# Attention over channels, then top-128 routing: batch 2's update taken before batch 3's gather, a weight load split unevenly, and a window of three on batch 3's stores

## The chip, the cores and the metric

The program runs on one core of one Trainium2 chip. The metric is the device time of one execution in microseconds (us). Before the change it is 260.9 us, the median of three runs (260.78 to 260.98). TensorE is PE in the rows, VectorE DVE, ScalarE ACT, GpSimd POOL, SyncE SP. DMAs are issued by POOL (loads, gathers, scatters) and by SP (weights, stores), and 16 DMA engines carry them.

## What is computed

Four batches of 6208 rows by 256 columns. For each batch the columns of q and k are scaled to length one, a 256x256 softmax is taken of the product of k and q over the rows, and v is multiplied by it. Then 128 rows of the result are chosen by a score and changed by a small MLP:

```python
qn = q / (norm(q, axis=1) + 1e-6);  kn = k / (norm(k, axis=1) + 1e-6)
a = softmax(kn.transpose(0, 2, 1) @ qn / tau)          # 256 x 256 for each batch
x = v @ a                                              # 6208 x 256
scores = x @ w_gate
for b in range(4):
    top = the 128 rows with the highest scores[b]
    ye = maximum(x[b, top] @ w1, 0) @ w2               # w1 256x1024, w2 1024x256
    out[b, top] = x[b, top] + sigmoid(scores[b, top]) * ye
```

All other rows of the output are x.

## The kernel before

Each batch is cut into six chunks of 1024 rows (128 partitions of 8 rows) and a rest of 64 rows, in the order 0, rest, 1 to 5. One chunk of q, k or v is a 1 MB load, cast to bf16 on the way. Batches are numbered 0 to 3; the code calls batch 2 `E` and batch 3 `L`. A batch passes through these steps:

- p1: matmuls over q and k give the norms (`p1_norms`, line 390, tile `g_ps`) and the product (`p1_rows`, line 401, `s_ps`); then the softmax (`softmax_stages`).
- T, S, O: each half chunk of v is transposed (`p2_transpose`, line 500, `vt_ps`), scored (`p2_score`, line 547, `sc_ps`) and multiplied by the softmax (`p2_out`, line 581; two rows a matmul group, copied to `stage` by ACT at line 599).
- Select: seven rounds on DVE and PE narrow a threshold (`select_stages`, lines 655 to 682), then the 128 row numbers come out (`idx`, line 735), POOL gathers those rows of v (line 741), PE transposes them (line 765, tile `vg`), the MLP runs (lines 775 to 830), and POOL scatters `upd` into the output (line 844). The scatter has to wait until the stores of its batch have landed.
- Two chunks of batch 2 (`LATE`, chunks 4 and 5) are treated otherwise: their O runs at the very end, with the MLP's change added by two more matmuls (line 588), so they need no scatter. Their stores wait for batch 2's scatter.

The order of the instructions is set at build time by a planner (the `while True` loop from line 942), which keeps model times for the engines (`Engines`) and the DMA queues (`Rings`) and takes, at each step, the ready piece of lowest priority number: chains (softmax, select, MLP), then S, then p1 and T, then O. Where PE would be idle, it puts in dummy matmuls (`unread`, line 533). A chain that has gathered asks `calm` whether it may go on; a chain that wants to scatter waits for `("stored", b)`. Stores that are ready before the loads have been issued are kept in `deferred`; the first of them waits for the load `GATE`, the first half of batch 3's last v chunk, and the others stand behind it in SP's order (lines 960 to 969). Each engine runs its instructions in the order written. DMAs of SP and of POOL each take turns over eight semaphores, so each waits for the landing of the one eight places ahead of it.

The w1, w2 and gate weights are loaded by SP at the start (lines 275 to 278) and cast by ACT once (lines 944 to 956).

Of the kernel before, what the change touches and what calls it, by code (L numbers as in the profile page):

```python
# [17 lines left out]
P = 128  # L18
# [7 lines left out]
FAR = 1.0e9  # L26
# [84 lines left out]
def kernel(  # L111
# [12 lines left out]
    nc = tc.nc  # L124
# [20 lines left out]
    VT_BUFS = 13  # L145
    AHEAD = 12.0

    const = ctx.enter_context(tc.tile_pool(name="const", bufs=1))
# [57 lines left out]
    def now():  # L206
        return eng.t["pe"]
# [51 lines left out]
    def pump():  # L259
        rings.run(now())  # L260
        flying[:] = [key for key in flying if rings.done.get(key, FAR) > now()]
        while nxt_unit[0] < len(units):
            u = units[nxt_unit[0]]
            if not slots[bucket(u)] or sum(length[key] for key in flying) >= AHEAD:
# [11 lines left out]
                      in_=moe_w1.rearrange("(dc p) f -> p dc f", p=P))  # L276
    nc.sync.dma_start(out=w2_st, in_=moe_w2.rearrange("(p fc) d -> p fc d", p=P))
    nc.sync.dma_start(out=wg_row, in_=moe_w_gate[None, :])
# [72 lines left out]
    late_add = []  # L351
    scatter_inst = {}
    gathered = set()
    softmaxes = [0]
# [265 lines left out]
    def select_stages(b, dep):  # L620
# [173 lines left out]
        sf = eng.dve(C, xf, extra=0.16)  # L794
        yield ("t", f)
        h_sb = moe.tile([P, NFC, P], BF16, name="h_sb")
        hfs = []
# [55 lines left out]
    def calm(b):  # L853
        if b == L:
            return True
        if b == E:
            return acc_dead[0]
        if softmaxes[0]:
            return False
        if acc_dead[0]:  # L860
            return True
        if not queue["T"]:
            return True
        u, g = queue["T"][0]
        return g != gs[0] or u not in loaded or rings.landing(arrival_key[u + (3,)]) > now() + 6.0

    class Chain:
# [7 lines left out]
        def ready(self):  # L875
            if self.need[0] == "t":
                return self.need[1]
            if self.need[0] == "dma":
                return rings.landing(self.need[1]) if calm(self.b) else FAR
            b = self.need[1]  # L880
            if held[b]:
                return FAR
            if b == L:
                return now()
            return max(rings.landing(key) for key in stored[b]) + (0.5 if L in gathered else 3.0)

# [30 lines left out]
    def stage_ready():  # L917
# [5 lines left out]
        return rings.landing(("st",) + key)  # L923

    def out_store(b, ci):
        dep = stage_done[(b, ci)]
# [5 lines left out]
        for h in range(parts):  # L932
            key = ("st", b, ci) if h == parts - 1 else ("st", b, ci, h)
            issued = eng.issue("sp", 0.42, dep)
            rings.add(1, issued + 0.65, STORE / parts + 0.009 if ci < NFULL else 0.2, key, 0.45)
            ins = emit_store(b, ci, h, parts)
        stored[b].append(key)
        if not late(b, ci):
# [3 lines left out]
    while True:  # L942
        pump()
        if not cast_done and now() > 8.0:
            w1v = w1_st.rearrange("p a c -> p (a c)").rearrange("p (dc m fc) -> p dc fc m", dc=C // P, fc=NFC)
# [11 lines left out]
        if nxt_unit[0] == len(units) and not drained and E in gathered:  # L957
            nc.gpsimd.drain(fusable=False)
            drained = True
        if deferred and GATE in load_inst:  # L960
            for b, ci in sorted(deferred, key=lambda d: -d[0]):
                st = out_store(b, ci)
                if not gate_done:
# [4 lines left out]
                        reason="stores behind the last loads")  # L968
            deferred = []
        t = now()  # L970
# [41 lines left out]
        if late_phase() and (queue["p1"] or queue["T"]):  # L1012
            coming = min([a[0] for a in able if a[1] == 2] + [FAR])
            fit = [a for a in fit if a[1] < 3 or coming > t + 0.44 + EARLY]
        if acc_dead[0]:
# [48 lines left out]
        else:  # L1064
# [8 lines left out]
            if out_at == len(outs) or outs[out_at][1][0] != g[0]:  # L1073
                if back(b, g[0]) and not gate_done:
                    deferred.append((b, g[0]))
                else:
                    out_store(b, g[0])
# [35 lines left out]
```

## Time and profile before

| | us |
|---|---|
| time, median of 3 | 260.9 |
| the profiled execution's own time | 260.56 |
| its span | 258.5 |
| PE busy | 214.4 (83%) |
| ACT busy | 94.5 |
| DVE busy | 98.9 |

HBM read 78.91 MB and written 25.95 MB. The span is the time from the program's first to its last instruction, 2.06 us less than the execution. The program can be read in three stretches: loads with the stores of batches 0 and 1 among them, up to about 217 us; stores of batches 1, 2 and 3 up to 255 us; and the last scatter with the end of the program. In a row of a timeline the columns are the start, the duration, engine, line, operation, the tiles written and read, the shape, the count, and in brackets how long the engine had been idle and what released it. A busy PE is not a PE at its peak, and a DMA share above 1 means that packets of one DMA engine overlap in the records.

### The profile page before, as it was taken

Reading aid. Unit: us, or ns where it says so; the run is one execution under the profiler, and the core shown is the slowest. Engines: PE = TensorE matmul, PEld = TensorE weight load, DVE = VectorE, ACT = ScalarE, POOL = GpSimd, SP = SyncE. Lnnn points to the kernel's source line nnn. Section 1 sums busy time; section 2 is a strip of 40 time slices with the busy share of each in tenths; the row PEclk is TensorE's granted clock in tenths of the full one; section 3 lists DMA queues with packets and bytes.
Section 4 is the critical chain, followed back from the end, with each engine's and each line's share of the span. In section 5 each row is a group of like instructions: output and inputs, shape, how many; then the busy total and the mean of one; then the engine's idle time right before and its main releaser. Section 6 shows DMA issues by size and latency. Waiting matters only on the chain.

```text
span 258.5 us, 8230 instructions
## 1 busy us (share of the span) xinstructions
PE 214.4 (83%) x3668; PEld 175.5 (68%) x3668; DVE 98.9 (38%) x417; ACT 94.5 (37%) x173; POOL 56.5 (22%) x105
## 2 busy tenths in 40 slices
PE   0396866898998995997958999899999889999960
PEld 0265655795876674786736788787878779887840
DVE  0200004367450055443663033556555256766030
ACT  2800004800116565457400021811022087698610
POOL 8241212223104110130104322123205300010201
PEclk9999799569999997999985999999999999999996
DMA  7999999999999999999999999999999996999995
GB/s 239 256 216 213 214 214 214 214 212 213 213 213 295 311 363 318 257 281 295 364 241 213 212 214 212 214 212 212 214 213 210 211 212 171 411 423 412 394 411 235
DMA packets 16852, 66.97 MB, mean 259 GB/s; under 512 B 2097, under 2 KB 3634, under 8 KB 13618
## 3 DMA queue, kind: packets, MB, share of 16 engines
q0 software_dynamic: 12528, 38.93, 75.5%
q1 hardware_dynamic: 4290, 27.53, 26.4%
q8 instruction: 28, 0.46, 0.6%
q14 instruction: 6, 0.05, 0.0%
HBM read 78.91 MB, written 25.95 MB: 406 GB/s over the span
## 4 chain that ended last, share of the span: by engine, by line
PE 48%; DMA 37%; DVE 6%; ACT 4%; issue 2%; POOLq 1%; POOL 0%; SPq 0%; DVEq 0%
DMA q_ch<-in_q_dram 17%; PE s_ps L401 12%; DMA k_ch<-in_k_dram 10%; PE o_ps L581 8%; PE g_ps L390 8%; DMA v_ch<-in_v_dram 7%; PE sc_ps L533 4%; DMA out_dram<-stage 3%; PE m_ps L673 3%; PE vt_ps L500 2%; PE sc_ps L547 2%; ACT stage L599 2%; PE s_ps L581 2%; DVE cmp L655 1%; PE g_ps L581 1%
## 5 line engine op out<-in xcount | busy, mean ns | idle before, releaser
L599 ACT COPY stage<-o_ps 128x512 f32<-128x512 f32 x78 | 43.8, 589 | 64.1 <-PE o_ps L581 62.9
L401 PE MATMUL s_ps<-q_ch,k_ch 128*128 128x256 bf16 x384 | 50.9, 287 | 0.0
L401 PEld LDWEIGHTS <-k_ch 128*128 128x128 bf16 x384 | 36.8, 102 | 6.3
L581 PE MATMUL o_ps<-a_sb,vt_sb 128*128 128x256 bf16 (+1 forms) x270 | 39.0, 274 | 2.6 <-ACT stage L599 2.5
L581 PEld LDWEIGHTS <-vt_sb 128*128 128x128 bf16 (+1 forms) x294 | 26.6, 98 | 8.9 <-issue 4.9
L500 PE MATMUL vt_ps<-ident_b,v_ch 128*128 128x128 bf16 x336 | 26.8, 236 | 2.8 <-DMA v_ch<-in_v_dram 1.9
L390 PE MATMUL g_ps<-q_ch 128*64 128x64 bf16 x768 | 18.5, 202 | 12.0 <-DMA q_ch<-in_q_dram 12.0
L500 PEld LDWEIGHTS <-v_ch 128*128 128x128 bf16 x384 | 25.1, 105 | 4.2 <-DMA v_ch<-in_v_dram 2.5
L390 PEld LDWEIGHTS <-q_ch 128*64 128x64 bf16 x768 | 15.1, 116 | 17.6 <-DMA q_ch<-in_q_dram 13.0
L415 DVE SCALAR_TENSOR_TENSOR junk<-g_ps,ident_h 128x64 f32<-128x64 f32 x16 | 3.6, 225 | 57.9 <-PE g_ps L390 57.5
L243 POOL DMA_DIRECT2D q_ch<-in_q_dram x25 | 13.9, 556 | 44.8 <-DMA q_ch<-in_q_dram 9.6
L519 DVE COPY vt_sb<-vt_ps 128x1024 bf16<-128x1024 bf16 x24 | 15.9, 689 | 20.1 <-PE vt_ps L500 20.1
L390 PE MATMUL g_ps<-k_ch 128*64 128x64 bf16 x768 | 18.1, 201 | 6.2 <-DMA k_ch<-in_k_dram 6.2
L390 PEld LDWEIGHTS <-k_ch 128*64 128x64 bf16 x768 | 15.0, 116 | 10.3 <-DMA k_ch<-in_k_dram 7.2
L243 POOL DMA_DIRECT2D v_ch<-in_v_dram x25 | 13.6, 546 | 34.6 <-DMA q_ch<-in_q_dram 19.2
L533 PE MATMUL sc_ps<-w_sb,ident_b 128*128 128x256 bf16 x134 | 20.3, 277 | 0.4 <-DVE sc L626 0.4
L243 POOL DMA_DIRECT2D k_ch<-in_k_dram x25 | 13.7, 547 | 28.8 <-DMA v_ch<-in_v_dram 13.4
L410 ACT COPY s_sb<-s_ps 128x512 f32<-128x512 f32 x4 | 2.3, 586 | 45.0 <-PE s_ps L401 45.0
L655 DVE SCALAR_TENSOR_TENSOR cmp<-sc,wl,tab 128x392 bf16<-128x392 f32 x28 | 17.5, 626 | 1.0
L844 POOL DMA_INDIRECT out_dram<-upd,idx x4 | 4.0, 997 | 49.3 <-DMA out_dram<-stage 49.0
L547 PEld LDWEIGHTS <-vt_sb 128*128 128x128 bf16 (+1 forms) x294 | 10.8, 100 | 5.0 <-issue 2.3
L547 PE MATMUL sc_ps<-aw_sb,vt_sb 128*128 128x2 bf16 (+1 forms) x294 | 11.7, 166 | 2.7 <-DVE aw_sb L479 2.6
(176 smaller groups left out, 261.4 us busy)
## 6 DMA issues: line engine op xcount, KB each, us to landing
out_dram<-stage SPq DMA_DIRECT2D x18, 1024.0 KB, 11.0
q_ch<-in_q_dram POOLq DMA_DIRECT2D x23, 512.0 KB, 16.9
k_ch<-in_k_dram POOLq DMA_DIRECT2D x23, 512.0 KB, 16.3
v_ch<-in_v_dram POOLq DMA_DIRECT2D x23, 512.0 KB, 17.8
out_dram<-stage SPq DMA_DIRECT2D x12, 512.0 KB, 8.9
stage<-in_moe_w_dram SPq DMA_DIRECT2D x2, 1024.0 KB, 5.0
q_ch<-in_q_dram POOLq DMA_DIRECT2D x2, 256.0 KB
k_ch<-in_k_dram POOLq DMA_DIRECT2D x2, 256.0 KB, 15.6
```

The lines of the kernel that those rows point to most:

```text
L243: ins = nc.gpsimd.dma_start(out=t[:, rows, :], in_=lview(src, b, d)[:, rows, :])
L390: nc.tensor.matmul(g_ps[h * H:(h + 1) * H, 2 * which + cc, :], lhsT=x, rhs=x, start=d == FIRST and s == 0 and cc == 0 and which == 0, stop ...
L401: nc.tensor.matmul(s_ps[:, cc, :], lhsT=kt[:parts, s, cc * P:(cc + 1) * P], rhs=qt[:parts, s, :], start=d == FIRST and s == 0 and cc == 0, ...
L500: nc.tensor.transpose(vt_ps[:, cc, j, :parts], in_=vt[:parts, v0 + j, cc * P:(cc + 1) * P], identity=ident_b[:parts, :parts])
L519: nc.vector.tensor_copy(vt_sb[:, :, :n, :parts], vt_ps[:, :, :n, :parts])
L533: nc.tensor.matmul(t[:, 256:512], lhsT=ident_b, rhs=w1_sb[:, 0, 0:256], start=not sc_open[0], stop=not sc_open[0])
L547: nc.tensor.matmul(sc_ps[:parts, col, :], lhsT=vt_sb[:, cc, j, :parts], rhs=aw_sb[:, cc, :], start=cc == 0 and col == 0, stop=cc == 1 and ...
L581: nc.tensor.matmul(o_ps[:parts, pj, :], lhsT=vt_sb[:, cc, j, :parts], rhs=a_sb[:, cc, :], start=pj == 0 and cc == 0, stop=last and cc == 1 ...
L599: nc.scalar.copy(st[:parts, rows, :], o_ps[:parts, :m, :])
L655: nc.vector.scalar_tensor_tensor(out=cmp, in0=sc[:, :, None].to_broadcast([P, NCOL, NTHR]), scalar=wl[:, i, NTHR:NTHR + 1], in1=tab[:, Non ...
L673: nc.tensor.matmul(mps[:, 0:7 * NTHR], lhsT=ones_b, rhs=cmp[:, 7 * h:7 * h + 7, :].rearrange("p s j -> p (s j)"), start=h == 0, stop=h == 6)
L844: ins = nc.gpsimd.indirect_dma_start(out=out_flat[0:(b + 1) * N, :], out_offset=bass.IndirectOffsetOnAxis(ap=idx[:, 0:1], axis=0), in_=upd ...
```

## The change

Five edits, all in the planner or at the start:

- The w2 load (1 MB) becomes one DMA of the first four of each partition's eight rows, and 16 DMAs of the other four rows with 8 partitions each (every fourth of 32 partitions). The planner puts the weights' casts at its 14 us instead of 8.
- `calm` lets batch 2's chain go on as soon as its gather has landed. A new stop, `("dead", f)`, holds it in front of the MLP's first weight until batch 3's p1 is done.
- Deferred stores are issued batch 2 first; batch 1's two follow when all of batch 2's (but the two late ones) have been issued.
- A batch before batch 2 doesn't scatter ahead of batch 3's gather once all loads are out; the allowance after the stores' landing is 1.5 us in the model for all.
- From the fourth on, each half store of a full chunk of batch 3 waits for the landing of the one three places ahead (`few`, `FEW = 3`, `after`).

```diff
+    UNEVEN = 4
...
-    nc.sync.dma_start(out=w2_st, in_=moe_w2.rearrange("(p fc) d -> p fc d", p=P))
+    w2v = moe_w2.rearrange("(p fc) d -> p fc d", p=P)
+    nc.sync.dma_start(out=w2_st[:, 0:NFC - UNEVEN], in_=w2v[:, 0:NFC - UNEVEN])
+    for p0 in [a + j for j in range(4) for a in range(0, P, P // 4)]:
+        ps = slice(p0, p0 + P // 4 - 3, 4)
+        nc.sync.dma_start(out=w2_st[ps, NFC - UNEVEN:], in_=w2v[ps, NFC - UNEVEN:])
...
         yield ("t", f)
+        if b == E:
+            yield ("dead", f)
         h_sb = moe.tile([P, NFC, P], BF16, name="h_sb")
...
         if b == E:
-            return acc_dead[0]
+            return True
...
+            if self.need[0] == "dead":
+                return self.need[1] if acc_dead[0] else FAR
...
-            return max(rings.landing(key) for key in stored[b]) + (0.5 if L in gathered else 3.0)
+            if b < E and L not in gathered and nxt_unit[0] == len(units):
+                return FAR
+            return max(rings.landing(key) for key in stored[b]) + 1.5
...
+    def after(later, earlier, reason):
+        tc.add_manual_dep(
+            later.ins, earlier.ins.name,
+            mybir.DependencyInfo(mybir.DependencyClass.Sync, mybir.DependencyReason.DATA), reason=reason)
...
             key = ("st", b, ci) if h == parts - 1 else ("st", b, ci, h)
+            if b == L and ci < NFULL and len(few) >= FEW:
+                dep = max(dep, rings.landing(few[-FEW][1]))
...
             ins = emit_store(b, ci, h, parts)
+            if b == L and ci < NFULL:
+                if len(few) >= FEW:
+                    after(ins, few[-FEW][0], "few stores at a time ahead of the last gather")
+                few.append((ins, key))
...
-        if not cast_done and now() > 8.0:
+        if not cast_done and now() > 14.0:
...
-        if deferred and GATE in load_inst:
-            for b, ci in sorted(deferred, key=lambda d: -d[0]):
+        if deferred and GATE in load_inst and (held[E] == 0 or any(b == E for b, _ in deferred)):
+            for b, ci in [d for d in deferred if d[0] == E] or list(deferred):
+                deferred.remove((b, ci))
                 st = out_store(b, ci)
...
-            fit = [a for a in fit if a[1] < 3 or coming > t + 0.44 + EARLY]
+            early = EARLY if not acc_dead[0] or len(queue["T"]) <= 3 else 0.0
+            fit = [a for a in fit if a[1] < 3 or coming > t + 0.44 + early]
...
-                if back(b, g[0]) and not gate_done:
+                if b < E and back(b, g[0]) or back(b, g[0]) and not gate_done:
                     deferred.append((b, g[0]))
```

What this does to the order is shown at three places. The first is SP's beginning, the weights; `stage` is their staging tile. Before:

```order
L275 DMA stage<-in_moe_w_dram 128x2x1024
L277 DMA stage<-in_moe_w_dram 128x2048
L278 DMA wg_row<-in_moe_w_gate_dram 1x256
L611 DMA out_dram<-stage 128x2048
L613 DMA out_dram<-stage_rem 64x256
```

Now:

```order
L276 DMA stage<-in_moe_w_dram 128x2x1024
L279 DMA stage<-in_moe_w_dram 128x1024
L282 DMA stage<-in_moe_w_dram 8x1024 x16
L283 DMA wg_row<-in_moe_w_gate_dram 1x256
L618 DMA out_dram<-stage 128x2048
```

The gate's row `wg_row` now stands behind 18 DMAs instead of two.

The second place is SP behind the last loads. The first row is batch 2's chunk 0, whose wait on `DMASW1` is the load `GATE`; `stage_2262` and `stage_2361` are batch 1's last two chunks before the change, `stage_2278` and `stage_2377` after it; 64x2048 is a half store of batch 3. Before:

```order
L611 DMA out_0_dram<-stage_3387 128x2048 [waits DMAHW7_49,DMASW1_49,Activation_49]
L613 DMA out_0_dram<-stage_rem_3876 64x256 [waits DMAHW0_49,Activation_49]
L611 DMA out_0_dram<-stage_3881 128x2048 [waits DMAHW1_49,Activation_49]
L611 DMA out_0_dram<-stage_2262 128x2048 [waits DMAHW2_49]
L611 DMA out_0_dram<-stage_2361 128x2048 [waits DMAHW3_49]
L611 DMA out_0_dram<-stage_4201 128x2048 [waits DMAHW4_49,Activation_49]
L611 DMA out_0_dram<-stage_4550 128x2048 [waits DMAHW5_49,Activation_49]
L611 DMA out_0_dram<-stage_4608 64x2048 [waits DMAHW6_49,Activation_49]
L611 DMA out_0_dram<-stage_4608 64x2048 [waits DMAHW7_49]
```

Now:

```order
L618 DMA out_0_dram<-stage_3897 128x2048 [waits DMAHW1_49,Activation_49]
L618 DMA out_0_dram<-stage_4232 128x2048 [waits DMAHW2_49,Activation_49]
L618 DMA out_0_dram<-stage_4483 128x2048 [waits DMAHW3_49,Activation_49]
L618 DMA out_0_dram<-stage_2278 128x2048 [waits DMAHW4_49]
L618 DMA out_0_dram<-stage_2377 128x2048 [waits DMAHW5_49]
L618 DMA out_0_dram<-stage_4606 64x2048 [waits DMAHW6_49,Activation_49]
L618 DMA out_0_dram<-stage_4606 64x2048 [waits DMAHW7_49]
L620 DMA out_0_dram<-stage_rem_4649 64x256 [waits DMAHW0_49,Activation_49]
L618 DMA out_0_dram<-stage_4669 64x2048 [waits DMAHW1_49,Activation_49]
L618 DMA out_0_dram<-stage_4669 64x2048 [waits DMAHW6_49,DMAHW2_49]
L618 DMA out_0_dram<-stage_4709 64x2048 [waits DMAHW7_49,DMAHW3_49,Activation_49]
```

Batch 2's four full chunks now go ahead of batch 1's two, and from the fourth half store of batch 3 each has a second DMA wait, on the half store three places ahead.

The third place is the end of POOL's order. The number of rows tells the scatters apart: 12416 is batch 1, 18624 batch 2, 24832 batch 3; the last `vg` is batch 3's gather. Before:

```order
L243 DMA v_ch<-in_v_dram 128x1024 x2
L844 DMA out_dram<-upd,idx 12416x256
L741 DMA vg<-in_v_dram,idx 128x256
L844 DMA out_dram<-upd,idx 18624x256
L844 DMA out_dram<-upd,idx 24832x256
```

Now:

```order
L244 DMA v_ch<-in_v_dram 128x1024 x2
L853 DMA out_dram<-upd,idx 18624x256
L748 DMA vg<-in_v_dram,idx 128x256
L853 DMA out_dram<-upd,idx 12416x256
L853 DMA out_dram<-upd,idx 24832x256
```

Batch 2's scatter now stands in front of batch 3's gather, and batch 1's behind it. On PE, batch 2's transposes of line 765 move ahead of the last eight matmuls of line 401, and between batch 3's last select matmul (line 727) and its line 765 there now stand seven O groups of batch 3 and seven late O groups of batch 2, where eight late O groups of batch 2 and twelve dummy matmuls stood before; the eighth late O group now comes right behind line 765.

## Rows read from the trace of the kernel before

**Rows 1.** The page: span, and DMA busy tenths in 40 slices.

```profile
span 258.5 us, 8230 instructions
...
DMA  7999999999999999999999999999999996999995
```

**Rows 2.** The page: the chain that ended last, by engine.

```profile
PE 48%; DMA 37%; DVE 6%; ACT 4%; issue 2%; POOLq 1%; POOL 0%; SPq 0%; DVEq 0%
```

**Rows 3.** Windows around the last loads; last three columns: PE clock, DMA share, GB/s.

```profile
213.00:214.00 1.00, 1.00 (x16) 0.94 (x15) 0.80 (x4) 1.00 (x2) 0.00 (x0) 1.00 1.08 211
214.00:215.00 1.00, 1.00 (x21) 1.00 (x19) 0.87 (x2) 1.00 (x3) 0.00 (x0) 1.00 0.64 129
215.00:216.00 1.00, 1.00 (x28) 0.96 (x27) 0.42 (x1) 1.00 (x4) 0.00 (x0) 1.00 0.62 113
216.00:217.00 1.00, 1.00 (x29) 0.95 (x29) 0.24 (x2) 0.69 (x3) 0.00 (x0) 1.00 0.57 107
217.00:218.00 1.00, 1.00 (x21) 0.95 (x19) 0.44 (x2) 0.00 (x0) 0.00 (x0) 1.00 0.19 35
218.00:219.00 1.00, 1.00 (x22) 1.00 (x20) 0.93 (x4) 0.72 (x1) 0.00 (x0) 1.00 0.67 268
```

**Rows 4.** Windows over the stores and at their end.

```profile
219.00:255.00 36.00, 30.57 (x365) 25.17 (x362) 16.54 (x64) 21.86 (x42) 3.97 (x4) 0.98 1.01 412
...
249.00:250.00 1.00, 0.92 (x14) 0.63 (x12) 0.75 (x2) 0.37 (x1) 0.00 (x0) 1.00 0.84 352
...
256.00:257.00 1.00, 0.00 (x0) 0.00 (x0) 0.00 (x0) 0.00 (x0) 0.00 (x0) 0.50 0.06 25
```

**Rows 5.** Timeline of SP's DMA issues, 216 to 260 us.

```profile
217.62 0.33 SPq L611 DMA_DIRECT2D out_dram<-stage  x1
...
230.22 19.81 SPq L611 DMA_DIRECT2D out_dram<-stage  x12
```

**Rows 6.** Landing of L611's stores issued at 217.6, then 236 to 238.5 us.

```profile
DMA to landing us min/median/max: 4.9/4.9/4.9
...
DMA to landing us min/median/max: 8.7/8.7/8.7
```

**Rows 7.** Timeline of POOL, 200 to 260 us, from the first scatter.

```profile
230.83 1.01 POOL L844 DMA_INDIRECT out_dram<-upd,idx  x1 [27.04 <-DMA out_dram<-stage]
238.78 0.99 POOL L741 DMA_INDIRECT vg<-in_v_dram,idx  x1 [6.94 <-DMA out_dram<-stage]
240.07 0.99 POOL L844 DMA_INDIRECT out_dram<-upd,idx  x1 [0.30 <-issue]
252.97 0.98 POOL L844 DMA_INDIRECT out_dram<-upd,idx  x1 [11.91 <-DMA out_dram<-stage]
```

**Rows 8.** Timeline of PE: two O groups, batch 3's gathered rows and its MLP's begin.

```profile
221.53 0.60 PE L581 MATMUL o_ps<-a_sb,vt_sb 128*128 128x256 bf16 x4
221.96 0.60 PE L581 MATMUL s_ps<-a_sb,vt_sb 128*128 128x256 bf16 x4
...
247.96 0.28 PE L765 MATMUL vt_ps<-ident_b,vg 128*128 128x128 bf16 x2 [1.91 <-DMA vg<-in_v_dram,idx]
...
248.63 0.38 PE L775 MATMUL m_ps<-vgt,a_sb 128*128 128x128 bf16 x4
```

**Rows 9.** Timeline of DVE: batch 3's row numbers, and its MLP's end.

```profile
238.35 0.15 DVE L735 TENSOR_SCALAR idx<-tok 128x1 int32<-128x1 f32 x1
...
252.04 0.48 DVE L830 SCALAR_TENSOR_TENSOR upd<-o_ps,gate,xe 128x256 f32<-128x256 f32 x1 [0.45 <-PE o_ps L826]
```

**Rows 10.** Chain in order of time, 236 to 260 us: the last store waited for.

```profile
244.65 7.18 DMA out_dram<-stage
```

**Rows 11.** SP's waits, 200 to 260 us: total, times, longest.

```profile
SPq L1108 <- DMA out_dram<-upd,idx: 7.1, 1, 7.1
SPq L611 <- DMA out_dram<-upd,idx: 3.1, 1, 3.1
```

**Rows 12.** Timeline of ACT, 0 to 60 us: w2's cast, and the next use of ACT but one.

```profile
10.48 1.90 ACT L949 CAST w_sb<-stage 128x2048 bf16<-128x2048 f32 x1 [0.71 <-DMA stage<-in_moe_w_dram]
...
41.66 0.59 ACT L410 COPY s_sb<-s_ps 128x512 f32<-128x512 f32 x1 [28.69 <-PE s_ps L401]
```

More of the change, by code (lines that the diff above doesn't have):

```diff
@@ L352 @@
     scatter_inst = {}
+    few = []
+    FEW = 3
     gathered = set()
@@ L968 @@
                         reason="stores behind the last loads")
-            deferred = []
         t = now()
```

## The prediction

> **What bounds the kernel now.** I read the page first: DMA is busy in tenths 9 in all but three of the 40 slices, the first, the 34th (6) and the last (5) [rows 1]. The chain is half PE, a third DMA [rows 2], but PE follows the loads, so time can only be won where DMA pauses, or behind its last byte. Then the windows: the pause lies between loads and stores. The DMA share falls from 1.08 to 0.64 at 214 us, stays at 0.62 and 0.57 for two more, and is 0.19 in 217 to 218 [rows 3]: some seven of the 16 DMA engines have ended their loads three microseconds before the others. The first store is issued at 217.62, when the first half of the last v chunk has landed [rows 5]. From 219 to 255 the share is 1.01 at 412 GB/s [rows 4].
>
> Last the tail, in three views. POOL issues batch 3's gather at 238.78 [rows 7], right behind the row numbers, which start at 238.35 [rows 9]; PE has waited 1.91 us when it transposes those rows at 247.96 [rows 8], 9.2 us after the issue. `upd` ends at 252.04 + 0.48 = 252.52 [rows 9] and the scatter starts at 252.97 [rows 7]. The store it also needs landed at 244.65 + 7.18 = 251.83 [rows 10]. So three things end together: the MLP (252.5), batch 3's stores (251.8), and the late stores behind them (DMA is down to 0.06 in 256 to 257 [rows 4]). To win, the change has to move all of them.
>
> **The change part by part.** Working is against the profiled execution, 260.56 us with a span of 258.5; the median, 260.9, is 0.34 above it, and the forecast is for the median.
>
> *w2 unevenly.* The bytes are the same. The split half is 128 partitions x 4 KB = 0.52 MB; at 412 GB/s [rows 4] it takes 1.27 us on 16 engines, so 2.54 on eight. If the 16 small DMAs fall on eight engines, these have 1.27 us more to do and the others 1.27 less. What remains at 214 us is (0.64 + 0.62 + 0.57 + 0.19) / 1.08 = 1.9 us of all engines [rows 3], so a perfect balance would end the loads near 216, some 1.5 us sooner than 217.5. The bounds are -1.27 (the eight are the early ones) and +1.27 (they are the late ones). I take -1.2: the shift, 2.5 us, is near the lead that the rows show.
>
> The trace doesn't say which engines lead. The Trainium skill, page "DMA: Bandwidth & Descriptors", section "Why a DMA increments its semaphore by 16 and not by 1", says that a DMA from SP whose slowest dimension is 8 runs on the eight lowest-numbered engines; by that the split does fall on one half, and no run here shows yet whether that is the early half.
>
> The 16 DMAs cost SP issue time at the start, and from the seventh each waits for a landing eight places ahead; behind them stands only the gate's row. The cover is ACT: it casts w2 at 10.48 and next needs to work at 41.66, but for one copy of the gate weights [rows 12]. A few microseconds there cost nothing. A PE that waits for the gate's row would hold up p1, which has DMA's queue ahead of it.
>
> The same page's "Rules for kernel authors" calls transfers under 64 KB mostly overhead, and these are 32 KB each; by that w2 lands late, which the 30 us of cover take.
>
> *Store order.* From 217.62 all stores together are bound by DMA: 36 us at 412 GB/s = 14.8 MB [rows 4]. Whatever starts them 1.2 us sooner ends them 1.2 us sooner. Queued on SP behind batch 2's chunks 2 and 3 are now batch 1's two, which need no more work. Chunk 3's last O comes near 223 (PE's O groups at 221.53 and 221.96 are its first two [rows 8]). Until then the chunks 0, 1 and 2 keep DMA: 3 x 2.55 us from 218.3 is 226. No hole: 0, and if the cover is gone, up to 1 us.
>
> *Batch 2's MLP and scatter.* The scatter stood behind batch 3's gather (240.07 [rows 7]); SP waited 3.1 us for it before it could issue the late stores [rows 11]. That wait goes. It hid little: the share was 0.84 in 249 to 250 [rows 4], a hole of 0.2 us. I take -0.1. Now the scatter needs its stores and batch 1's two, seven DMAs, landed by about 234 to 236, and POOL's 1.0 us for it, before the row numbers at 238.5: two microseconds of room. PE is full from 213 to 218 [rows 3] and on to the last score, so loads that land sooner don't speed the scores; the moved pieces (matmuls of lines 765, 775, 780) are the same work earlier, and they close a gap in PE's softmax stretch. I take -0.3 for the row numbers, bounds -0.8 and +0.5.
>
> *Window of three.* A 1 MB store on an idle queue lands 4.9 us after its issue, one with eight in flight 8.7 [rows 6]. A half on an idle queue takes 4.9 - 1.27 = 3.6; three take 3.8 us of DMA. So three are just enough to keep DMA busy: 0. The other bound: if a half in a window of three took 4.9 us, one would pass every 1.63 us instead of 1.27, and the nine that wait would lose 9 x 0.36 = 3.2 us.
>
> For the gather the window takes four or five halves out of the way: 9.2 - 4 x 1.27, about 4 to 5 us. But PE's order doesn't let that count. Between line 727 and batch 3's line 765 stand seven O groups of 0.43 (221.96 - 221.53 [rows 8]) and seven late ones of twice that: 3.0 + 6.1 = 9.1 us. Line 727 ends 1.05 us before the gather's issue (the row numbers lie between), so line 765 runs 8.1 to 8.3 us after it instead of 9.2. One late group (0.87) then stands before line 775, which hitherto came 0.67 us after line 765 [rows 8] by two short steps. Net: -0.4, bounds 0 and -0.9. From 775 the rest is unchanged.
>
> Batch 1's scatter, moved behind the gather, stands in front of batch 3's by twelve microseconds: 0.
>
> Sum: `upd` and with it the scatter -0.3 - 0.4 = -0.7, to 252.3; batch 3's last store -1.2, to 250.6; the late stores -1.3. The scatter starts at 252.3 with less traffic before it, which gives 0.2 to 0.3 back: the end moves by -0.9. 260.56 - 0.9 = 259.7; for the median **260.0 us**.
>
> **Rivals.**
>
> 1. The load's end doesn't move: one late engine is among those that take w2, or the small DMAs spread over all 16. For it: "some seven" leave nine late ones, more than half, so at least one late engine may get more. Against it: the split is over rows, 8 a DMA. Then the late stores end where they did, and only the scatter's -0.7 counts until it meets them, within 0.3: 260.6.
> 2. The eight are the late ones: load end and all stores +1.2, and the wait for batch 3's stores becomes the scatter's: 262.1. Nothing in the rows excludes it.
> 3. Slower by the window: a half's landing, issue to semaphore, takes longer than 3 x 1.27 = 3.8 us, the point from which DMA runs dry between halves on the engine that is last. For it: 8.7 us with eight in flight is not far over twice the idle 3.6. Against it: the 3.6 itself. At 4.5 us the loss is 9 x 0.23 = 2.1, less the 1.2 of w2: 261.8.
> 4. The window doesn't do what it says: the gather's 9.2 us are not the stores' doing. For it, the Trainium skill ("DMA: Bandwidth & Descriptors", "Queues, rings and completion order"): a DMA engine goes round its queues packet by packet, and by that a gather would not stand behind eight stores. The rows speak against it: a gather takes 9.2 us beside stores, and a scatter that starts after most of them is over by 257, 4 us after its issue [rows 4, 7]. If the gather still takes 9.2, line 765 waits 1 us longer than PE's order asks and 0.5 of the gain is lost: 260.3.
>
> **How the numbers follow.** Forecast 0.45 (259.3 to 260.4), rival 1 0.27, rival 4 0.08, rival 3 0.13, rival 2 0.07. A measurement here can tell 0.2%, 0.52 us: faster means under 260.38, slower over 261.42. The forecast gives 0.40 of faster, rival 1 0.07, rival 4 0.05: 0.52. Slower: most of rivals 2 and 3 and a little of the rest: 0.20. Same: 0.28. The range leaves out the worst of rivals 2 and 3 at the top and, below, a case where balance and gather both reach their better ends (-1.5 and -0.9): 258.8 to 261.7.
>
> **What would show it.** In the windows the DMA share should fall in one microsecond at the loads' end instead of four, and SP's first store behind the loads start near 216.4. SP's halves should land under 5 us after their issue, with the DMA share near 1.0 from 235 to 248; a share of 0.8 to 0.9 there is rival 3. POOL's scatter of batch 2 should start before 237, PE's line 765 run 8 us after the gather's issue with no wait for DMA in front of it, and the late stores be issued without a wait for a scatter. A first store at 217.6 is rival 1, at 218.8 rival 2. The prediction is wrong in kind if the row numbers come over 1 us later or sooner than 238.3, since then PE's stretch from 205 to 223 decides, and not DMA.

## The result and the profile after

The changed kernel takes 262.8 us (median of 10 runs, 261.46 to 264.44) against 260.69 us for the kernel before (260.40 to 260.98): it is slower, ratio 1.0073 with a 95% interval of 1.0057 to 1.0089. That lies outside the predicted 258.8 to 261.7. A trace is of one execution (those of the kernels without the window, with the uneven load alone and with seven alone below are of their slowest, 262.72, 262.83 and 263.62 us), and the ratios come from all undisturbed runs, not from the medians. Here the profiled execution took 262.84 us. First the page of the changed kernel: its span, 2.6 us longer than before, DMA's 40 slices, the instruction fetches among the DMA queues, and the chain by engine.

```profile
span 261.1 us, 8265 instructions
...
DMA  6999999999999999999999999999999994999995
...
q8 instruction: 28, 0.46, 0.6%
...
PE 50%; DMA 34%; DVE 7%; ACT 4%; issue 2%; POOLq 1%; POOL 0%; SPq 0%; DVEq 0%
```

The page looks as in [rows 1, 2], with the pause in the 34th slice deeper (4 in place of 6). Here are the windows around the last loads, as in [rows 3]; DMA share and GB/s are the last two columns.

```profile
213.00:214.00 1.00, 1.00 (x17) 0.94 (x15) 0.84 (x5) 1.00 (x5) 0.00 (x0) 1.00 1.00 195
214.00:215.00 1.00, 1.00 (x15) 0.93 (x13) 0.89 (x5) 1.00 (x3) 0.00 (x0) 1.00 1.04 195
215.00:216.00 1.00, 1.00 (x35) 0.97 (x32) 0.95 (x3) 1.00 (x3) 0.00 (x0) 1.00 1.00 188
216.00:217.00 1.00, 1.00 (x28) 0.86 (x26) 0.93 (x4) 0.68 (x1) 0.00 (x0) 1.00 0.43 80
217.00:218.00 1.00, 1.00 (x27) 1.00 (x24) 1.00 (x3) 0.00 (x0) 0.00 (x0) 1.00 0.17 33
218.00:219.00 1.00, 1.00 (x24) 0.92 (x20) 0.88 (x2) 0.33 (x1) 0.00 (x0) 1.00 0.14 27
219.00:220.00 1.00, 1.00 (x24) 0.98 (x22) 0.04 (x1) 0.85 (x2) 0.00 (x0) 1.00 0.15 33
```

The step of 0.6 from 214 to 217 is gone: most engines now end together, near 216. But a tail of 0.14 to 0.17 is left, the work of two to three engines of sixteen, and lasts past 219. The stores wait for it. Next SP's issues and batch 3's two last links in the chain of waits (start and duration; the chain's pieces between them are left out).

```profile
219.51 0.33 SPq L618 DMA_DIRECT2D out_dram<-stage  x1
...
232.05 20.61 SPq L618 DMA_DIRECT2D out_dram<-stage  x12
```

```profile
246.50 3.95 DMA out_dram<-stage
...
250.47 4.05 DMA out_dram<-stage
```

The first store is 1.89 us later than in [rows 5]. Batch 3's last half lands at 250.47 + 4.05 = 254.52, 2.69 later than the 251.83 of [rows 10]: 0.8 was lost after the start of the stores. The windows show where, in two stretches of five microseconds behind batch 1's stores, in which the kernel before has shares of 1.03 and 1.04 at 418 and 390 GB/s:

```profile
235.00:240.00 5.00, 4.78 (x52) 3.74 (x50) 3.21 (x18) 3.71 (x7) 1.08 (x2) 1.00 0.91 367
240.00:245.00 5.00, 5.00 (x48) 4.47 (x47) 1.38 (x2) 3.47 (x7) 1.91 (x2) 1.00 0.96 352
```

POOL, DVE and PE in batch 3's tail, answering to [rows 7, 8, 9]:

```profile
238.61 1.01 POOL L853 DMA_INDIRECT out_dram<-upd,idx  x1 [32.83 <-DMA out_dram<-stage_rem]
239.92 0.99 POOL L748 DMA_INDIRECT vg<-in_v_dram,idx  x1 [0.30 <-issue]
...
255.66 0.98 POOL L853 DMA_INDIRECT out_dram<-upd,idx  x1 [11.00 <-issue]
```

```profile
239.14 0.15 DVE L742 TENSOR_SCALAR idx<-tok 128x1 int32<-128x1 f32 x1
...
252.06 0.48 DVE L839 SCALAR_TENSOR_TENSOR upd<-o_ps,gate,xe 128x256 f32<-128x256 f32 x1 [0.45 <-PE o_ps L835]
```

```profile
247.66 0.28 PE L772 MATMUL vt_ps<-ident_b,vg 128*128 128x128 bf16 x2
```

The row numbers and the gather are 0.8 and 1.1 us later than before, and yet `upd` ends at 252.54, within 0.02 of its time before: the gather's delay was taken up by PE's order, and line 772 waits for nothing. The last scatter starts at 255.66 in place of 252.97, not for `upd` but for the store that landed at 254.52, 1.14 before it. The same 1.14 lay between the store of [rows 10] (251.83) and the scatter of [rows 7], so the store, and not the MLP, held the scatter before the change too. The end, 261.1, is 5.4 us behind it, as before (258.5 - 252.97 = 5.5). SP's wait of 3.1 us for a scatter [rows 11] is gone; in its place SP waits for the landing of stores, 6.3 us in seven waits, the longest 1.5:

```profile
SPq L618 <- DMA out_dram<-stage: 6.3, 7, 1.5
```

### The profile page after: what moved, and what is told of

It is laid out like the page before. It is cut to its first block, busy times and chain, and to the rows that moved or that the text cites. A ratio compares the mean times of both kernels' runs of the same rounds, so it can differ in the third digit from the quotient of the medians.

```text
span 261.1 us, 8265 instructions
## 1 busy us (share of the span) xinstructions
PE 215.3 (82%) x3672; PEld 175.4 (67%) x3672; DVE 101.7 (39%) x421; ACT 91.6 (35%) x169; POOL 56.5 (22%) x105
## 4 chain that ended last, share of the span: by engine, by line
PE 50%; DMA 34%; DVE 7%; ACT 4%; issue 2%; POOLq 1%; POOL 0%; SPq 0%; DVEq 0%
PE s_ps L408 14%; DMA q_ch<-in_q_dram 10%; PE g_ps L397 9%; PE o_ps L588 8%; DMA v_ch<-in_v_dram 7%; DMA k_ch<-in_k_dram 7%; DMA stage<-in_moe_w_dram 5%; PE sc_ps L540 4%; DMA out_dram<-stage 3%; PE m_ps L680 3%; DVE cmp L662 2%; PE vt_ps L507 2%; PE sc_ps L554 2%; DMA wg_row<-in_moe_w_gate_dram 2%; ACT stage L606 2%
## 5 line engine op out<-in xcount | busy, mean ns | idle before, releaser
L408 PE MATMUL s_ps<-q_ch,k_ch 128*128 128x256 bf16 x384 | 51.5, 288 | 0.0
L397 PE MATMUL g_ps<-q_ch 128*64 128x64 bf16 x768 | 19.1, 205 | 10.8 <-DMA q_ch<-in_q_dram 10.7
L507 PE MATMUL vt_ps<-ident_b,v_ch 128*128 128x128 bf16 x336 | 24.9, 226 | 2.3 <-DMA v_ch<-in_v_dram 1.6
L397 PEld LDWEIGHTS <-q_ch 128*64 128x64 bf16 x768 | 15.8, 119 | 15.7 <-DMA q_ch<-in_q_dram 11.4
L507 PEld LDWEIGHTS <-v_ch 128*128 128x128 bf16 x384 | 23.5, 100 | 3.7 <-DMA v_ch<-in_v_dram 2.3
L397 PE MATMUL g_ps<-k_ch 128*64 128x64 bf16 x768 | 18.8, 205 | 4.2 <-DMA k_ch<-in_k_dram 4.2
L540 PE MATMUL sc_ps<-w_sb,ident_b 128*128 128x256 bf16 x138 | 21.7, 277 | 0.4 <-DVE sc L633 0.4
L397 PEld LDWEIGHTS <-k_ch 128*64 128x64 bf16 x768 | 15.8, 119 | 8.2 <-DMA k_ch<-in_k_dram 4.9
```

The source lines that it names most:

```text
L397: nc.tensor.matmul(g_ps[h * H:(h + 1) * H, 2 * which + cc, :], lhsT=x, rhs=x, start=d == FIRST and s == 0 and cc == 0 and which == 0, stop ...
L408: nc.tensor.matmul(s_ps[:, cc, :], lhsT=kt[:parts, s, cc * P:(cc + 1) * P], rhs=qt[:parts, s, :], start=d == FIRST and s == 0 and cc == 0, ...
L507: nc.tensor.transpose(vt_ps[:, cc, j, :parts], in_=vt[:parts, v0 + j, cc * P:(cc + 1) * P], identity=ident_b[:parts, :parts])
L540: nc.tensor.matmul(t[:, 256:512], lhsT=ident_b, rhs=w1_sb[:, 0, 0:256], start=not sc_open[0], stop=not sc_open[0])
```

## Experiments

Each kernel was timed against the kernel before (260.5 to 260.7 us in these comparisons). Two suspects stand at the loads' end (theories G and U), one in the tail (theory W). At the start, PE's timeline shows a long stand for the gate's row, and ACT's for w2:

```profile
14.39 1.89 PE L408 MATMUL s_ps<-q_ch,k_ch 128*128 128x256 bf16 x8
21.59 1.19 PE L976 MATMUL m_ps<-wg_row,ones_f 1*128 1x256 f32 x2 [5.32 <-DMA wg_row<-in_moe_w_gate_dram]
```

```profile
20.94 1.90 ACT L973 CAST w_sb<-stage 128x2048 bf16<-128x2048 f32 x1 [11.28 <-DMA stage<-in_moe_w_dram]
```

Theory G takes the loads' delay for the work of this stand; theory U for that of the extra bytes on engines that were late already; theory W takes the rest for the window's.

**The gate's row first.** On SP alone:

```diff
+    nc.sync.dma_start(out=wg_row, in_=moe_w_gate[None, :])
     w2v = moe_w2.rearrange("(p fc) d -> p fc d", p=P)
...
-    nc.sync.dma_start(out=wg_row, in_=moe_w_gate[None, :])
```

> The changed kernel with one move on SP: the gate's row is loaded second, ahead of w2's 17 DMAs, and no other engine's order differs. Theory G (PE stands 5.3 us in batch 0's p1 for the gate's row, frees its q and k buffers late, and so the loads are late): the 5.3 us go, the first store behind the last loads starts at 217.6 or sooner in place of 219.5, time 260.7 to 261.2. Rival U (the 16 small DMAs lay 1.27 us on engines that are late anyway): PE's wait goes too, but the first store starts at 218.8 or later and the time is 262.2 or more.

Measured: 262.95 us, ratio 1.0087 (1.0063 to 1.0112). PE's stand is gone, the first store is not sooner:

```profile
16.01 1.22 PE L976 MATMUL m_ps<-wg_row,ones_f 1*128 1x256 f32 x2
```

```profile
219.53 0.33 SPq L618 DMA_DIRECT2D out_dram<-stage  x1
```

Theory G, which the chain of waits had suggested (5.48 us of it pass through `wg_row`), falls: the first store is at 219.51 with the stand and at 219.53 without it. That the loads POOL had already issued cover a stand of 5 us is the likely reason.

**w2 in one DMA.** The uneven part is taken back (and the cast put at 8.0 again):

```diff
-    nc.sync.dma_start(out=w2_st[:, 0:NFC - UNEVEN], in_=w2v[:, 0:NFC - UNEVEN])
-    for p0 in [a + j for j in range(4) for a in range(0, P, P // 4)]:
...
+    nc.sync.dma_start(out=w2_st, in_=moe_w2.rearrange("(p fc) d -> p fc d", p=P))
```

> The changed kernel with w2 loaded by one DMA and cast as before; the rest of the change stays. Both theory G and rival U: first store at 217.6, as in the kernel before. If the window of three costs nothing, the time is then 260.0 to 260.5; if it costs what the tail seems to show (L's last half lands 2.7 us later while the first store is only 1.9 later, so 0.8), 261.0 to 261.5. If neither the start nor the loads matter: 262.8.

Measured: 260.99 us, ratio 1.0024 (1.0010 to 1.0037), first store at 217.57, as both theories said.

```profile
217.57 0.33 SPq L614 DMA_DIRECT2D out_dram<-stage  x1
```

The uneven load costs 1.8 us here; what is left is still slower than before by 0.24%, at the edge of what was expected of a window that costs.

**The window away.**

```diff
-    FEW = 3
+    FEW = 99
```

> The changed kernel without the waits of batch 3's half stores on the one three places ahead; no engine's order differs. Theory W (the window stretches the nine halves from 1.27 to 1.45 us each): the halves flow at about 1.3 us, the last lands about 1 us sooner (253.5), the gather takes over 8 us again and PE's line 772 runs up to 1 us later; the last scatter starts between 253.5 and 254.5, time 261.5 to 262.0. Rival (the loads' end alone makes the loss, the window is free): 262.6 to 263, and if the gather's gain is real, 263 or more.

Measured: 261.43 us, ratio 1.0033 (1.0020 to 1.0045), first store at 219.26: 1.4 us under the changed kernel, slightly better than theory W asked for. The window is the second loss.

**The uneven load alone**, in the kernel before, with the cast at 14:

```diff
-    nc.sync.dma_start(out=w2_st, in_=moe_w2.rearrange("(p fc) d -> p fc d", p=P))
+    nc.sync.dma_start(out=w2_st[:, 0:NFC - UNEVEN], in_=w2v[:, 0:NFC - UNEVEN])
+    for p0 in [a + j for j in range(4) for a in range(0, P, P // 4)]:
...
```

> The kernel before with the uneven w2 load and its later cast alone. Theories G and U both: first store 1.5 to 2 us later than 217.6, the whole tail with it, time 262.2 to 262.8. If the loads' lateness came from the other parts of the change (batch 2's MLP in PE's stretch from 205 to 217): 260.0 to 260.9 with a first store at 217.6 or sooner.

Measured: 262.09 us, ratio 1.0055 (1.0036 to 1.0073), first store at 219.44, with a tail of 0.22 and 0.14 after 217.

```profile
219.44 0.33 SPq L616 DMA_DIRECT2D out_dram<-stage  x1
```

The loads' lateness is this edit's, with nothing else of the change there; the time was 0.1 us under what was expected.

**Seven engines, sixteen engines.** If one of the eight engines is the late one, leaving out the last may spare it; and 16 partitions a DMA show whether small DMAs as such are the trouble. In place of the loop over 8 partitions, in the changed kernel, for seven (first line) and for sixteen (second line):

```diff
+    for ps in [slice(p0, p0 + 6 * 18 + 1, 18) for p0 in range(18)] + [slice(126, P)]:
...
+    for ps in [slice(p0, p0 + 15 * 8 + 1, 8) for p0 in range(8)]:
```

> The changed kernel with the second half of w2 in 18 DMAs of 7 partitions and one of 2, in place of 16 of 8; no other engine's order differs. After the split over 8 the DMA share falls at 216 us, but 0.14 to 0.17, two or three engines' worth, is left to 219.5. Theory U (one of the eight engines that take the split is a late one, and gets 1.27 us more): with seven it gets 1.27 us less, the share falls to nothing near 216.5, the first store starts at 216.3 to 217.0 and the time is 259.8 to 260.6. Rival (the stragglers are other engines, or small DMAs as such make the loads late): first store at 219 or later, time 262.5 or more.

> The changed kernel with the second half of w2 in 8 DMAs of 16 partitions. Theory U: the bytes fall on all 16 engines again, the DMA share has its step of 0.6 from 214 to 217 as in the kernel before, first store at 217.6, time 260.8 to 261.3, like w2 in one DMA. Rival (many small DMAs at the start are what costs): first store at 218.5 or later, time 262 or more.

Measured: seven 262.76 us, ratio 1.0081 (1.0061 to 1.0100), first store 219.78, the same tail: the eighth is not the engine, or not the only one, that is late. Sixteen 262.06 us, ratio 1.0059 (1.0044 to 1.0074), first store 217.75, and the old step is back one microsecond later:

```profile
214.00:215.00 1.00, 1.00 (x11) 0.90 (x10) 0.83 (x7) 1.00 (x3) 0.00 (x0) 1.00 1.03 199
215.00:216.00 1.00, 1.00 (x27) 0.97 (x26) 0.98 (x3) 1.00 (x3) 0.00 (x0) 1.00 0.63 119
216.00:217.00 1.00, 1.00 (x28) 0.98 (x27) 0.91 (x3) 1.00 (x2) 0.00 (x0) 1.00 0.56 104
217.00:218.00 1.00, 1.00 (x24) 0.86 (x22) 0.97 (x3) 0.10 (x1) 0.00 (x0) 1.00 0.38 70
```

So it is where the bytes go, not the number of DMAs, that moves the loads' end by two microseconds. The time missed its 260.8 to 261.3, though: it is 1.1 us over w2 in one DMA, with the same first store within 0.2, and no run settles why. The Trainium skill, page "DMA: Bandwidth & Descriptors", section "Why a DMA increments its semaphore by 16 and not by 1", says that a DMA from SP uses the largest count up to 16 that divides its slowest dimension, from the lowest engine on. The shapes of the tail with 8 and with 16 agree with that. The Trainium skill, same page, section "Latency and other measured facts", calls engines 7 and 15 usually the slow ones. By that order a split over the lowest seven leaves engine 7 out, and it was as slow (first store 219.78), so here others are late.

**Seven alone**: the loop over 7 partitions in the kernel before, with the gate's row ahead of it as in the first experiment:

> The kernel before with w2's second half in 18 DMAs of 7 partitions and one of 2, the gate's row loaded ahead of them, and the later cast; nothing else of the change. Theory U: the loads of all engines end near 216.2, first store 216.3 to 217.0 in place of 217.6, all stores about 1 us sooner, time 259.4 to 260.0. Rival: 262 or more, like the split over eight.

Measured: 262.10 us, ratio 1.0060 (1.0040 to 1.0080), first store 220.20: the rival, a second time.

**Neither split nor window** (the second and the third experiment's diffs together). What is left is batch 2's moved work with the order of the stores, and the `early` margin:

> The changed kernel with w2 in one DMA and without the window of three: what is left is batch 2's MLP, stores and scatter moved forward. Theory W (the window costs 0.6 to 1.4 us): the halves of batch 3 flow at 1.3 us each, the last lands near 251.8, time 259.9 to 260.4. Rival (the window pays for itself by the gather, and batch 2's scatter in front of the gather is what costs): batch 3's gather is issued over 1 us behind its row numbers and takes over 8 us, time 261 or more.

Measured: 260.34 us, ratio 0.9994 (0.9985 to 1.0002): no change that can be told from none. Against w2 in one DMA with the window, 260.99, the window costs 0.65. DMA in 235 to 240 shows it, first with the window of three, then without it, then with six in flight:

```profile
235.00:240.00 5.00, 4.78 (x49) 4.15 (x49) 2.75 (x11) 3.97 (x8) 1.99 (x2) 1.00 0.85 333
```

```profile
235.00:240.00 5.00, 4.78 (x48) 3.94 (x46) 2.81 (x14) 4.00 (x8) 1.99 (x2) 1.00 1.02 416
```

```profile
235.00:240.00 5.00, 4.78 (x48) 3.94 (x46) 2.75 (x13) 3.73 (x8) 1.99 (x2) 1.00 1.02 416
```

At 333 in place of 416 GB/s five microseconds carry 1.0 us less. The half stores from 238 to 249 take, from issue to landing, with three in flight and with six:

```profile
DMA to landing us min/median/max: 4.3/4.4/4.6
```

```profile
DMA to landing us min/median/max: 7.8/8.0/8.8
```

Three halves of 1.27 us are 3.8 us of work, and each takes 4.4 to come back. The kernel with six:

```diff
-    FEW = 3
+    FEW = 6
```

> The changed kernel with w2 in one DMA and a window of six half stores in place of three. Theory W (three in flight, each 4.3 to 4.5 us from issue to landing, pass one half every 1.45 us; with six in flight DMA has always work): halves at 1.3 us, the last lands as without the window, the gather takes 6 to 8 us; time 260.2 to 260.5. Rival (the loss is in the waits themselves, whatever their number): 260.9 to 261.2 as with three.

Measured: 260.48 us, ratio 0.9991 (0.9982 to 0.9999). Six in flight cost nothing, so it is the depth that costs, not the wait. The gather takes 8.7 us without the window (the first row below), 3.9 with three (the second, of the changed kernel with the gate's row first). With six its landing is not on record, but PE waits 0.91 us for it and starts 8.9 us after its issue, where 6 to 8 was expected.

```profile
DMA to landing us min/median/max: 8.7/8.7/8.7
```

```profile
DMA to landing us min/median/max: 3.9/3.9/3.9
```

The window does what it says, but it has little use. By its own order PE gets to those rows 7.7 us after the gather's issue, so only the 0.5 us that it waits for the gather without the window (0.9 with six) can be won; and the last scatter stands behind the stores. With w2 in one DMA and the window `upd` ends at 250.33, yet the scatter starts at 253.23, 1.14 behind this store (248.46 + 3.63 = 252.09):

```profile
248.46 3.63 DMA out_dram<-stage
```

**Four engines, two engines.** In the kernel before, two of w2's eight rows a partition in one DMA of 124 partitions (4 x 31) and one of 4; or one row in one of 122 (2 x 61) and three of 2. By the order above these run on four engines and on two:

```diff
+    nc.sync.dma_start(out=w2_st[:, 0:6], in_=w2v[:, 0:6])
+    for ps in (slice(0, 124), slice(124, P)):
+        nc.sync.dma_start(out=w2_st[ps, 6:], in_=w2v[ps, 6:])
...
+    nc.sync.dma_start(out=w2_st[:, 0:7], in_=w2v[:, 0:7])
+    for ps in (slice(0, 122), slice(122, 124), slice(124, 126), slice(126, P)):
+        nc.sync.dma_start(out=w2_st[ps, 7:], in_=w2v[ps, 7:])
```

> The kernel before with the last two of w2's eight rows a partition (0.26 MB) in a DMA of 124 partitions and one of 4, by the page's rule on four DMA engines; every order is as before but for SP's three w2 DMAs. By 412 GB/s the four get 1.9 us more, the other twelve 0.64 less. Theory U4 (the two late engines of the split are not among these four): the loads end 0.6 us sooner, first store 217.0, time 260.0 to 260.4. Rival (one or both are): first store at 219 to 219.5, time 261.8 to 262.5.

> The kernel before with the last of w2's eight rows a partition (0.13 MB) in one DMA of 122 partitions and three of 2, by the page's rule on two DMA engines: 2.2 us more for these, 0.3 less for the others. If neither of the two is a late one: first store 217.3 to 217.6, time 260.3 to 260.7. If one is: first store at 219.5 or later, time 262 or more, and only one engine's worth of DMA share left at the end.

Measured: four 260.50 us, ratio 0.9994 (0.9986 to 1.0003), first store 217.36: none of the four is a late one, though half the expected 0.6 is missing and the time is 0.1 over what was expected. Two 267.69 us, ratio 1.0261 (1.0229 to 1.0293), for another reason than either theory's: PE stood 19 us for the gate's row, which had come behind the pieces on those engines; POOL's next load waited 20.7 us for PE; and DMA's share fell to 0.20 (rows in this order).

```profile
30.12 1.19 PE L955 MATMUL m_ps<-wg_row,ones_f 1*128 1x256 f32 x2 [18.99 <-DMA wg_row<-in_moe_w_gate_dram]
```

```profile
35.93 0.53 POOL L243 DMA_DIRECT2D q_ch<-in_q_dram  x1 [20.69 <-PE s_ps L404]
```

```profile
32.00:36.00 4.00, 4.00 (x54) 2.93 (x50) 0.00 (x0) 0.00 (x0) 0.07 (x1) 1.00 0.20 39
```

**Five, six.** In the kernel before, the gate's row second, two rows of eight: 125 partitions (5 x 25) and 3; or 114 (6 x 19), 6, 6 and 2.

```diff
+    for ps in (slice(0, 125), slice(125, P)):
...
+    for ps in (slice(0, 114), slice(114, 120), slice(120, 126), slice(126, P)):
```

> The kernel before with the last two of w2's rows a partition in one DMA of 125 partitions and one of 3, by the page's rule on five DMA engines (1.4 us more for these, 0.64 less for the others), and the gate's row loaded second. If the fifth engine is not a late one: first store 217.0 to 217.4, time 260.0 to 260.6. If it is: first store 218.5 or later, time 261.4 or more.

> The same with 114 partitions, two DMAs of 6 and one of 2: by the rule on six engines, 1.1 us more for these, 0.64 less for the others. If neither the fifth nor the sixth is late: first store 217.0 to 217.4, time 260.0 to 260.6, and the seventh is the late one. If one is: 218.3 or later, 261.2 or more.

Measured: five 260.17 us, ratio 0.9985 (0.9976 to 0.9995), first store 216.82. Six 260.96 us, ratio 1.0017 (1.0002 to 1.0032), first store 217.98, between the two expectations. The last loads with five, and then with six:

```profile
215.00:216.00 1.00, 1.00 (x15) 0.93 (x13) 0.93 (x5) 1.00 (x3) 0.00 (x0) 1.00 0.91 170
216.00:217.00 1.00, 1.00 (x21) 1.00 (x19) 0.70 (x2) 1.00 (x4) 0.00 (x0) 1.00 0.56 111
217.00:218.00 1.00, 1.00 (x29) 0.98 (x26) 0.59 (x1) 1.00 (x4) 0.00 (x0) 1.00 0.56 199
```

```profile
216.00:217.00 1.00, 1.00 (x12) 0.89 (x10) 0.91 (x5) 1.00 (x2) 0.00 (x0) 1.00 0.74 137
217.00:218.00 1.00, 1.00 (x21) 1.00 (x19) 0.66 (x3) 1.00 (x3) 0.00 (x0) 1.00 0.17 37
218.00:219.00 1.00, 1.00 (x25) 1.00 (x23) 0.89 (x2) 1.00 (x4) 0.00 (x0) 1.00 0.32 127
```

With five no tail is left (the 0.56 at 199 GB/s in 217 to 218 is the stores' begin); with six it is back. By the order in which the engines are taken, the sixth and the seventh are the late ones among the lowest eight.

The traces bear this out one landing at a time. The semaphore of a load is raised sixteen times, as it seems once for each engine, and a trace keeps the sixteen moments. For `GATE`, the load that the first store waits for, they lie in the kernel before at 212.96 to 215.04 (eight), 216.31 to 216.53 (seven) and 217.57 (one alone). With w2 over four engines four early ones are left, at 212.30 to 212.87; over five with three rows (below) three are, at 212.33 to 212.61. Over six, one stands behind all others (217.93, the next at 216.87); over seven, two (218.67 and 219.73, the next at 217.18); over eight again two (218.50 and 219.46, the next at 216.74). So the first five are early, the sixth and the seventh late, and the eighth is not.

**Without the window, w2 steered.** The changed kernel with four, with four and the gate's row second, with five, and with five and three rows of eight (the same lines of diff as above; in the last, five rows go in one DMA and three are steered):

> The changed kernel without the window and with w2 steered as in the run over four engines. Theory U4: 0.6 us under the same kernel with w2 in one DMA (260.34), 259.6 to 260.0. Rival: 261.5 to 262.2.

> The changed kernel without the window, w2 steered to four engines, and the gate's row loaded second. In the same kernel with the gate's row last PE stood 8.8 us in batch 0's p1. If that stand delays loads at all: under 260.16 by 0.2 or more, 259.6 to 260.0. If DMA's queue covers it, as in the changed kernel with the row moved: 260.1 to 260.3.

> The changed kernel without the window, the gate's row second, and two of w2's rows steered to five DMA engines. If the steering to five adds to batch 2's moved work: first store 216.8, 0.5 us under the same kernel with one w2 DMA (260.34), 259.6 to 260.0. If the tail is by now held by batch 3's MLP: 260.0 to 260.3, like four.

> The same with three of w2's rows (0.39 MB): 2.1 us more for five engines, 0.95 less for the others. If all five have the lead of three microseconds that the step in the DMA share shows: first store 216.4 to 216.8, 259.4 to 260.0. If one of them has less: first store later than with two rows, 260.3 or more.

Measured: 260.16 us, ratio 0.9978 (0.9968 to 0.9989); 260.01, 0.9976 (0.9964 to 0.9988); 259.98, 0.9978 (0.9969 to 0.9987); 260.27, 0.9992 (0.9982 to 1.0003). The first misses its 259.6 to 260.0 by 0.16. The first three beat both kernels, the one before by 0.2%, and can't be told apart: the 8.8 us that PE stands in the first cost nothing, and the half microsecond by which five starts the stores sooner (216.96 against 217.51 with four) is not in the time. In the one with five `upd` ends at 252.67 + 0.48 = 253.15, since the row numbers came 2.3 us later than in the same kernel with w2 in one DMA, and the scatter, at 253.44, waits for it; why PE is late there is open.

```profile
252.67 0.48 DVE L838 SCALAR_TENSOR_TENSOR upd<-o_ps,gate,xe 128x256 f32<-128x256 f32 x1 [0.45 <-PE o_ps L834]
```

With three rows the first store is at 217.56: by its expectation one of the five has less lead than 2.1 us, so the lead can't be used in full. Which one is not shown.

## Why the prediction was wrong, step by step

**w2, the step that failed.** The reading of [rows 3] was right in kind: some engines end three microseconds before the others, and bytes shifted to them level the step. Wrong was the next step, "I take -1.2", which took the eight engines of the split for the early ones: two of the eight are late. Loads end with their last engine. By the working these two got +1.27, its outer bound; measured, the loads' end moved by +1.8 to +1.9 instead of -1.2 (first store 219.51 against 217.57, 219.44 against 217.62, 219.26 against 217.40). In time that is +1.1 to +1.8 (262.8 against 260.99, 262.09 against 260.66, 261.43 against 260.34). Where the 0.6 beyond the bound comes from is not shown. Rival 1 named the condition, "at least one late engine may get more", and drew the wrong result from it, a loads' end that doesn't move; rival 2's price, +1.2, lies within what was measured, and it needs one late engine among the eight, not eight. So rival 2's 0.07 was far too little: rival 1's condition, held for 0.27, is enough for it.

**The window, the second step that failed.** The working had the numbers: 3.6 us for a half on an idle queue against 3.8 us of work in a window of three, and took "just enough" for 0. Measured: 4.3 to 4.6 us for a half, DMA at 0.85 to 0.91 from 235 to 240, and 0.65 us (260.99 against 260.34) to 1.4 us (262.8 against 261.43). That is rival 3's mechanism, with a price under its 2.1. The row of a store alone on an idle queue bounds the landing of one between two others from below, and it was taken for its value.

**Both at once.** Rivals 2 and 3 don't exclude each other, but each was priced alone, at 262.1 and at 261.8 (this with w2's 1.2 as a gain). Over the kernel with neither (260.34) the uneven load alone costs 1.1 and the window alone 0.65, which would make 262.1; with both it is 262.8. The last 0.7 comes only with the two together, and no run shows how.

**Why eight engines lead.** The prediction said that the trace doesn't tell which engines lead. The sixteen raises do tell how the lead came about. In the kernel before they lie within 0.4 us of each other until the first instruction fetch, at 18.9 us. Behind it one comes 1.2 us after the first, behind the second fetch (27.8) two, and so on to eight, 1.1 to 1.3 late, behind the eighth (74.4). Behind the sixteenth (149.6) eight are 2.3 to 2.5 late, behind the twenty-fourth (203.7) 3.3 to 3.5, and behind the next (214.2) one alone is 4.6 late. So each fetch, a packet of 16 KB that takes 0.9 us, sets one engine back by 1.0 to 1.2 us; by the counts the fetches go round the same eight engines, and these don't catch up before the loads end. In the changed kernel eight raises are 2.9 to 3.2 late at 22 us, before any fetch, from w2's uneven half; of the first seven fetches two hit these (4.5 late at 76.7) and five the others (1.2 to 1.7). From there on two stay last: the stragglers of the loads' end. No run changed the fetches; the cause is read from the order of events.

**Batch 2's moved work.** Worth little, as forecast: with the stores' order but neither split nor window it gives 260.34, -0.2 us in the median. Its scatter started at 236.5 there, and the row numbers were 0.85 sooner, just past the working's bound of 0.8. `upd` ended 0.97 sooner (251.55), but the last scatter started only 0.32 sooner (252.65), for it follows the store. The sum, which let the scatter start behind `upd`, had that path wrong. In the changed kernel the late loads brought the scatter to 238.6, beside the row numbers, and the two microseconds of room were gone.

**The gather and PE's order.** Right in kind: 247.66 - 239.92 = 7.7 us where 8.1 to 8.3 was forecast, without a wait for DMA. PE's own way, from the last select matmul's end (238.54) to line 772, is 9.12 us where the working had 9.1; the gather was issued 0.3 later behind that matmul than assumed. That the landing came down to 3.9 us refutes rival 4.

**PE behind the gate's row** was named as a hazard and priced at nothing: right at 5 and at 9 us of standing, wrong at 19.

**Open.** Besides what is called not shown above: why the changed kernel's runs spread over 3 us, and why eight DMAs over all sixteen engines cost 1.1 us although the loads ended within 0.2 us of their time.

## What to carry to other kernels

A transfer that all engines share ends with its last engine: before bytes are shifted between engines, find out which ones are late, one by one, since a mean share shows how many lead but not which. A window of in-flight stores has to be sized by the landing measured in the loaded stretch (three were too few here, six enough; four and five were not run); and a wait that is shortened is worth nothing where the engine behind it comes later by its own order. When two mishaps don't exclude each other, the forecast needs a case for both; here it cost more than the sum of the two.

## What was not expected of the hardware

A DMA's number of partitions chose the engines it ran on closely enough to steer by: two rows of w2 over 4, 5 and 6 engines put the first store at 217.36, 216.82 and 217.98, four rows over 7, 8 and all 16 at 219.78, 219.51 and 217.75. An instruction fetch of 16 KB set one DMA engine back by some 1.1 us, and 24 of them put eight engines 3.3 to 3.5 us behind. And PE standing still for 9 us near the start cost nothing, while in the run where it stood 19 us the load queue ran empty and the time was 7 us longer.
